# Attention and GEGLU backward, one decode step: weight rows put side by side in a partition, and what follows from it

## The chip, the cores and the metric

The kernel runs on one core of one Trainium2 chip. The time is the device time of one execution in microseconds (us), median of several executions. Engines as the profile names them: PE is the matrix engine (PEld its weight loads), DVE the vector engine, ACT the scalar engine, POOL the GpSimd engine, SP the engine that here only issues transfers. Transfers issued by SP show as queue q1, by ACT as q10, by POOL as q0.

## What is computed

The reference is one decode step of a block with attention and a GEGLU feed-forward side by side, and its gradients by the inputs and weights. The shapes: batch B = 4, D = 512, 32 query heads and 8 key/value heads of 128, a cache of 4096 positions of which the last W = 1024 are seen, F = 1792, all in bf16.

```python
xn = layernorm(x)                                  # x: [4, 1, 512]
q = (xn @ wq) as [4, 32, 1, 128]                   # wq: [512, 4096]
p = softmax(q @ k[:, :, -1024:].T * 128**-0.5)     # each kv head serves 4 query heads
o = p @ v[:, :, -1024:]
out = x + o @ wo + (gelu(xn @ w_gate) * (xn @ w_up)) @ w_down    # wo: [4096, 512]
# and, for grad_out dy: dx, dk_cache, dv_cache, dwq, dwo, dw_gate, dw_up, dw_down
```

The outputs are out (out_0), dx (out_1), dk and dv (out_2, out_3, both of the full cache's size, zero outside the window), dwq (out_4), dwo (out_5), dw_gate, dw_up, dw_down (out_6 to out_8). With do = dy @ wo.T by heads, dv comes from p and do, dp from do and v, dq from the scores' gradient and k, and dwo is the outer product of o and dy. 30.93 MB are read and 81.01 MB written, most of the latter the zeros of out_2 and out_3.

## The kernel before, in words

Weights and caches come into SBUF by SP (`load_w`, L228; `load_kv`, L235). The constants are made first: `xnT` and `dyT` (L204 to L210) hold the normalised x and dy with D on the partitions, in ND = 4 chunks of 128; chunk c holds the rows c*128 to c*128+127. `xnm` and `dym` (L213 to L218) hold xn and dy four times, each time with all but one row of each batch's 32-row group masked out; with them as an operand one matmul forms the outer product for one of the four heads of a group.

The feed-forward part runs first (L531 to L659): w_down transposed block by block for the gradient of the hidden layer, gate and up, the GELU's derivative, then w_gate and w_up transposed for dx. Outer products for the weight gradients are put as small pieces into a deque `bg`; `tick(n)` takes n pieces from it, and is called inside the loops, so that matmuls, evictions and stores of one part lie between those of the next. A piece is a matmul into a PSUM tile of pool `ps_w` (four slots, shared by nearly all tiles), an eviction by `evac` (L84), which picks ACT or DVE by a running account of costs, and after the last piece of a buffer a store issued by POOL.

Attention runs in NT = 4 stages t (L669 to L687), each with two kv heads, that is, HG = 8 query heads and CW = 1024 columns of w_q and rows of w_o. In a stage:

- `pre(t)` (L280) forms do and q for the stage. It transposes w_o in blocks (`woT_ps`, evicted by DVE as `woT`), multiplies them with `dyT` into `doq_ps` (L293), multiplies w_q with `xnT` into the other half of `doq_ps` (L298), spreads both (L305, L307) and transposes them back to rows (L313).
- `masks(t)` spreads these rows by batch on POOL.
- `scores(t, 0)` and `scores(t, 1)` (L327) transpose k and v blocks on PE (`T_ps`, evicted by DVE as `T_sb`) and form the scores and dp (`S_ps`, L341); `softmax`, `softmax_d` follow.
- `dvdk(t, k)` (L432) puts the pieces for dv and dk into `bg`.
- `odq(t, k)` (L408) forms o (k = 0) or dq (k = 1) in `od_ps`, evicts the rows (L421, L423), transposes them (L426) and copies the transposed (L428). For the next stage `pre(t + 1)` stands between `odq(t, 0)` and `odq(t, 1)`.
- `fin(t)` (L497) adds o @ w_o to the output's sum and dq @ w_q.T to that of dx, transposing w_q in blocks (L508).
- `load_next(t)` (L242) issues the loads of stage t + 2, whose w_o and w_q take the place of those that `fin(t)` has just read.
- `dw(t)` (L455) puts the pieces for dwo (`piece_o`) and dwq (`piece_q`) into `bg`.

The zeros of out_2 and out_3 are stored by ACT's queue from one zero tile, some at each of several places (`zeros`, L253).

The order on SP is the program's order; on the other engines a planner orders the instructions by priority and its own costs, and adds the waits. Two engines that use one PSUM tile are made to wait for each other.

How the rows of a weight lie on the partitions is set by the views of the loads, such as

```python
wo_v = A_wo.rearrange("(t h p) n -> t p h n", p=P, h=HG)         # L221
wq_v = A_wq.rearrange("(c p) (t j) -> t p c j", p=P, j=CW)       # L222
```

Partition p of w_o's tile holds the rows p, p + 128, ... p + 896 of the stage, eight runs of 1 KB; that of w_q four runs of 2 KB, that of w_gate and w_up four of 3.5 KB.

Of the kernel before, what the change touches and what calls it, by code (L numbers as in the profile page):

```python
# [14 lines left out]
P = 128  # L15
# [3 lines left out]
def kernel(  # L19
# [23 lines left out]

    nc = tc.nc
# [21 lines left out]
    assert Sq == 1 and Dh == P and D == 512 and F % P == 0 and RG == 32 and JQ * NQ == J and WQ == JQ * P  # L66
# [53 lines left out]
    nc.sync.dma_start(out=wg_sb[:], in_=B_w_gate.rearrange("(c p) f -> p c f", p=P))  # L120
    wu_sb = ffn_w.tile([P, ND, F], BF16, name="wu_sb")
    nc.sync.dma_start(out=wu_sb[:], in_=B_w_up.rearrange("(c p) f -> p c f", p=P))
# [83 lines left out]
    for src, dstT in ((dy_b, dyT), (xn_b, xnT)):  # L206
        tps = ps_x.tile([P, ND, P], BF16, name="tps", tag="x")
        for c in range(ND):
            nc.tensor.transpose(tps[:, c, :], src[:, c * P:(c + 1) * P], ident[:])
        nc.vector.tensor_copy(out=dstT[:], in_=tps[:].rearrange("p c (b r) -> p c b r", b=B)[:, :, :, 0])  # L210
# [3 lines left out]
    dym = const.tile([P, rep, D], BF16, name="dym")  # L214
# [6 lines left out]
    wo_v = A_wo.rearrange("(t h p) n -> t p h n", p=P, h=HG)  # L221
    wq_v = A_wq.rearrange("(c p) (t j) -> t p c j", p=P, j=CW)  # L222
# [57 lines left out]
    def pre(t):  # L280

        wo_sb, wq_sb = wo_t[t], wq_t[t]
        dq_ps = ps_x.tile([P, 2, HG, B], FP32, name="doq_ps", tag="x")
        for h2 in range(HG // 2):
# [6 lines left out]
            for i in range(2):  # L291
                for c in range(ND):
                    nc.tensor.matmul(dq_ps[:, 0, 2 * h2 + i, :], lhsT=woT[:, i, c, :], rhs=dyT[:, c, :],  # L293
                                     start=(c == 0), stop=(c == ND - 1))
            tick(2)
        for h in range(HG):
            for c in range(ND):
                nc.tensor.matmul(dq_ps[:, 1, h, :], lhsT=wq_sb[:, c, h * Dh:(h + 1) * Dh], rhs=xnT[:, c, :],  # L298
                                 start=(c == 0), stop=(c == ND - 1))
        T4 = []  # L300
        for k, (sc, zt, nm) in enumerate(((None, dom_all[t % 2], "do"), (scale, qm_all[t % 2], "qs"))):
            xT4 = attw.tile([P, NQ, B, HG], BF16, name=nm + "T4", tag=nm + "T4")
            src = dq_ps[:, k].rearrange("p h b -> p b h").unsqueeze(1).broadcast_to([P, NQ, B, HG])
# [104 lines left out]
    def odq(t, k):  # L408
# [10 lines left out]
        rows = attw.tile([P, GP, Dh], BF16, name="od_r", tag=f"od_r{k}")  # L419
        if k == 0:  # L420
            nc.vector.tensor_copy(out=rows[:], in_=od_ps[:, k])  # L421
        else:
            nc.scalar.activation(out=rows[:], in_=od_ps[:, k], func=ACT.Copy, scale=scale)  # L423
# [3 lines left out]
        rT = attw.tile([P, GP, rep, B], BF16, name="od_T", tag=f"od_T{k}")  # L427
        nc.vector.tensor_copy(out=rT[:],  # L428
                              in_=T_ps[:].rearrange("p g (b r) -> p g r b", b=B)[:, :, 0:rep, :])
        st[t][("o", "dq")[k]] = rows, rT  # L430
# [24 lines left out]
    def dw(t):  # L455

        o_r, dq_r = st[t]["o"][0], st[t]["dq"][0]

        def piece_o(g, i, held):
# [3 lines left out]
            nc.tensor.matmul(mps[:], lhsT=o_r[:, g, :], rhs=dym[:, i, :], start=True, stop=True)  # L463
            evac(held["osb"][:, i, :], mps[:], 512)
            if i == rep - 1:
                r0 = (t * HG + g * rep) * Dh
                store(nc.gpsimd, out=out_5[r0:r0 + rep * Dh, :].rearrange("(h p) n -> p h n", p=P),
                                    in_=held["osb"][:], kind="rest",
                          apart=["zeros", "rest"])

        def piece_q(c2, k, held):
# [5 lines left out]
            for i in range(2):  # L477
                nc.tensor.matmul(mps[:, i].rearrange("p g d -> p (g d)"),  # L478
                                 lhsT=xnm[:, i2 * 2 + i, c * P:(c + 1) * P],
                                 rhs=dq_r[:].rearrange("p g d -> p (g d)"), start=True, stop=True)  # L480
            evac(held["osb"][:, ci, :, i2 * 2:(i2 + 1) * 2, :], mps[:].rearrange("p i g d -> p g i d"), 512)
            if k == 3:
                store(nc.gpsimd, out=out_4[c2 * 2 * P:(c2 + 1) * 2 * P, t * CW:(t + 1) * CW].rearrange("(c p) j -> p c j", p=P),
# [13 lines left out]
    def fin(t):  # L497
# [3 lines left out]
        acc_sum(0, [(lambda c, h=h: wo_sb[:, h, c * P:(c + 1) * P], oT[:, h // rep, h % rep, :]) for h in range(HG)])  # L501
# [114 lines left out]
    def piece_g(s_r, og, c, i, held):  # L616
# [4 lines left out]
        nc.tensor.matmul(mps[:, 0:n, :].rearrange("p f d -> p (f d)"), lhsT=xnm[:, i, c * P:(c + 1) * P],  # L621
                         rhs=s_r[:, 0:n, :].rearrange("p f d -> p (f d)"), start=True, stop=True)
        evac(held["osb"][:, 0:n, i, :], mps[:, 0:n, :], n * P)
        if i == 3:
            store(nc.gpsimd, out=og[c * P:(c + 1) * P, :],
# [36 lines left out]
    with tc.tile_pool(name="stage", bufs=3, reuse_waits="tile") as stage, \  # L662
# [32 lines left out]
        for o in range(2):  # L695
# [3 lines left out]
            fin_ps.append(f_ps[:].rearrange("p c d -> p (c d)"))  # L699
        acc_o, acc_d = fin_ps  # L700
# [51 lines left out]
```

## Time and profile before

| | us |
|---|---|
| median of 3 runs (lowest, highest) | 290.51 (288.97, 291.4) |
| the profiled execution's own time | 289.23 |
| its span, first to last instruction | 287.5 |

| engine | busy us | share of the span |
|---|---|---|
| PE | 206.9 | 72% |
| PEld | 141.5 | 49% |
| DVE | 144.9 | 50% |
| ACT | 113.7 | 40% |
| POOL | 66.7 | 23% |

112.38 MB pass through the 16 DMA engines, 391 GB/s over the span; the mean granted clock of PE is 0.849 of full speed.

How to read the lines that follow: a group's line has line, engine, operation, output <- inputs, shape, count, then busy us and mean ns of one, then the idle time of the engine just before and what ended it. The chain that ended last is followed back from the end: each piece is what released the next. A window's line has the busy us and the number of instructions of each engine in that stretch, the granted PE clock, the share of the DMA engines and GB/s. A share slightly over 1 is counted where packets overlap.

### The profile page before, as it was taken

How to read it: one execution, taken by the hardware profiler on the slowest of the kernel's cores; microseconds unless marked ns; L12 is line 12 of the kernel's file. 1: busy time of each engine (PE TensorE's matmuls, PEld its weight loads, DVE VectorE, ACT ScalarE, POOL GpSimd, SP SyncE). 2: the span in 40 equal slices, each digit the busy share in tenths (PEclk: the TensorE clock that was granted, in tenths of full speed). 3: DMA queues.
4: the chain of work that ended last, by engine and by line, in shares of the span. 5: the costliest groups of instructions: out<-in, count | busy, mean ns of one | idle time of the engine just before them, and what ended most of it. 6: DMA issues, size and time to landing. Idle time of an engine off the chain costs nothing.

```text
span 287.5 us, 6821 instructions
## 1 busy us (share of the span) xinstructions
PE 206.9 (72%) x2956; PEld 141.5 (49%) x2956; DVE 144.9 (50%) x310; ACT 113.7 (40%) x217; POOL 66.7 (23%) x84
## 2 busy tenths in 40 slices
PE   1397994983977999545689996546998679597710
PEld 0386882652644765333357654323665355364310
DVE  5484572333564567312626674126476525537770
ACT  1201653443442467312424563134355444336610
POOL 7000130441303152311033323110252132112410
PEclk9996899597897899795958898959799969959975
DMA  5999999999999999999998999999999999999897
GB/s 138 381 389 376 385 399 421 413 403 429 423 426 427 413 372 401 435 415 427 416 419 330 327 363 429 426 427 411 415 413 380 395 390 412 406 415 360 337 393 295
DMA packets 30182, 112.38 MB, mean 391 GB/s; under 512 B 1537, under 2 KB 7689, under 8 KB 26057
## 3 DMA queue, kind: packets, MB, share of 16 engines
q10 hardware_dynamic: 4612, 50.46, 41.9%
q1 hardware_dynamic: 17732, 30.81, 29.4%
q0 software_dynamic: 7808, 30.67, 27.3%
q8 instruction: 23, 0.38, 0.5%
q14 instruction: 7, 0.05, 0.0%
HBM read 30.93 MB, written 81.01 MB: 389 GB/s over the span
## 4 chain that ended last, share of the span: by engine, by line
PE 47%; DMA 28%; DVE 14%; issue 4%; ACT 2%; POOL 1%; SPq 0%; DVEq 0%; ACTq 0%; POOLq 0%
DMA out_dram<-osb_o 14%; PE T_ps L336 9%; PE kv_ps L444 7%; DMA out_dram<-stg_dv 4%; DVE T_sb L94 4%; PE S_ps L341 4%; DMA wd_sb<-in_B_w_down_dram 4%; DMA out_dram<-osb_d 3%; PE od_ps L416 3%; PE woT_ps L288 3%; PE wqT_ps L508 3%; DMA out_dram<-osb_g 2%; PE acc_ps L181 2%; PE wgT_ps L648 2%; PE wdT_ps L536 2%
## 5 line engine op out<-in xcount | busy, mean ns | idle before, releaser
L94 DVE COPY T_sb<-T_ps 128x1024 bf16<-128x1024 bf16 x64 | 44.2, 691 | 34.2 <-PE T_ps L336 33.7
L92 ACT CAST stg_dv<-kv_ps 128x512 bf16<-128x512 f32 x52 | 28.8, 589 | 43.2 <-PE kv_ps L444 42.8
L92 ACT CAST stg_dk<-kv_ps 128x512 bf16<-128x512 f32 x46 | 25.0, 588 | 15.4 <-PE kv_ps L444 13.1
L336 PE MATMUL T_ps<-ident,vb 128*128 128x128 bf16 x256 | 26.1, 251 | 6.6 <-DVE osb_q L94 6.6
L336 PEld LDWEIGHTS <-vb 128*128 128x128 bf16 x256 | 20.0, 114 | 12.7 <-issue 8.9
L92 ACT CAST osb_q<-dwq_ps 128x512 bf16<-128x512 f32 x25 | 13.6, 589 | 30.4 <-DMA out_dram<-osb_o 20.1
L336 PE MATMUL T_ps<-ident,kb 128*128 128x128 bf16 x256 | 24.4, 228 | 0.5 <-ACT stg_dk L92 0.3
L336 PEld LDWEIGHTS <-kb 128*128 128x128 bf16 x256 | 18.1, 101 | 12.4 <-issue 5.0
L444 PE MATMUL kv_ps<-domr,P_q 128*128 128x512 bf16 x64 | 23.9, 435 | 0.0
L444 PE MATMUL kv_ps<-qmr,dS_q 128*128 128x512 bf16 x64 | 20.9, 410 | 1.5 <-ACT stg_dk L92 1.0
L92 ACT CAST osb_g<-dwg_ps 128x384 bf16<-128x384 f32 (+1 forms) x30 | 14.5, 534 | 17.6 <-PE dwg_ps L621 8.1
L94 DVE COPY woT<-woT_ps 128x1024 bf16<-128x1024 bf16 x16 | 11.1, 692 | 17.2 <-PE woT_ps L288 17.2
L478 PE MATMUL dwq_ps<-od_r,xnm 128*128 128x256 bf16 x64 | 12.5, 320 | 6.8 <-DVE osb_q L94 6.6
L352 POOL TENSOR_TENSOR dS_q<-dS_b,qmsk 128x1024 bf16<-128x1024 bf16 x4 | 7.5, 1884 | 34.3 <-DVE dS_b L405 34.3
L92 ACT CAST osb_o<-dwo_ps 128x512 bf16<-128x512 f32 x23 | 12.7, 588 | 7.0 <-PE dwo_ps L463 6.8
L341 PE MATMUL S_ps<-T_sb,dom 128*32 128x256 bf16 x128 | 10.5, 310 | 5.1 <-DVE T_sb L94 5.1
L98 POOL DMA_DIRECT2D out_dram<-osb_q x8 | 5.8, 731 | 34.6 <-ACT osb_q L92 34.6
L94 DVE COPY wqT<-wqT_ps 128x1024 bf16<-128x1024 bf16 x16 | 11.0, 687 | 5.5 <-PE wqT_ps L508 5.3
L508 PEld LDWEIGHTS <-wq_sb 128*128 128x128 bf16 x128 | 11.1, 120 | 5.3 <-issue 4.3
L94 DVE CAST osb_q<-dwq_ps 128x512 bf16<-128x512 f32 x7 | 4.7, 689 | 16.9 <-DMA out_dram<-osb_o 16.9
L98 POOL DMA_DIRECT2D out_dram<-stg_dv x8 | 6.2, 774 | 30.4 <-ACT stg_dv L92 30.4
L94 DVE CAST stg_dk<-kv_ps 128x512 bf16<-128x512 f32 x18 | 12.0, 685 | 2.4 <-PE kv_ps L444 1.2
(187 smaller groups left out, 381.1 us busy)
## 6 DMA issues: line engine op xcount, KB each, us to landing
out_dram<-ztile ACTq DMA_DIRECT2D x8, 3072.0 KB, 16.5
out_dram<-ztile ACTq DMA_DIRECT2D x16, 1536.0 KB, 15.3
kb<-in_A_k_cache_dram SPq DMA_DIRECT2D x8, 1024.0 KB, 17.1
vb<-in_A_v_cache_dram SPq DMA_DIRECT2D x8, 1024.0 KB, 49.5
out_dram<-stg_dv POOLq DMA_DIRECT2D x8, 1024.0 KB, 10.1
out_dram<-stg_dk POOLq DMA_DIRECT2D x8, 1024.0 KB, 8.4
wo_sb<-in_A_wo_dram SPq DMA_DIRECT2D x4, 1024.0 KB, 10.2
wq_sb<-in_A_wq_dram SPq DMA_DIRECT2D x4, 1024.0 KB, 14.2
```

Source lines behind the costliest of these rows:

```text
L92: last.append(nc.scalar.copy(out=out, in_=in_))
L94: return nc.vector.tensor_copy(out=out, in_=in_)
L98: d = eng.dma_start(out=out, in_=in_)
L181: nc.tensor.matmul(ps[:, c, :], lhsT=lf(c), rhs=rhs, start=(k == 0), stop=(k == len(terms) - 1))
L288: nc.tensor.transpose(wT_ps[:, i, c, :], wo_sb[:, 2 * h2 + i, c * P:(c + 1) * P], ident[:])
L336: nc.tensor.transpose(T_ps[:, j, :], blks[(t, g)][:, b, j, :], ident[:])
L341: nc.tensor.matmul(ps[q * RG:(q + 1) * RG, :], lhsT=lf[:, s * RG:(s + 1) * RG], rhs=T_sb[:, q * WQ:(q + 1) * WQ], start=(g == 0 and b == 0 ...
L352: nc.gpsimd.tensor_tensor(out=dst[:], in0=src[:].unsqueeze(1).broadcast_to([P, NQ, WQ]), in1=qmsk[:].unsqueeze(2).broadcast_to([P, NQ, WQ] ...
L416: nc.tensor.matmul(od_ps[b * RB:b * RB + rep, k, g, :], lhsT=pT[:, jj, c0:c0 + rep], rhs=blks[(t, g)][:, b, j, :], start=(j == 0), stop=(j ...
L444: nc.tensor.matmul(mps[:].rearrange("p b d -> p (b d)"), lhsT=src[:, q, jj * P:(jj + 1) * P], rhs=mr[:, g].rearrange("p b d -> p (b d)"), ...
L478: nc.tensor.matmul(mps[:, i].rearrange("p g d -> p (g d)"), lhsT=xnm[:, i2 * 2 + i, c * P:(c + 1) * P], rhs=dq_r[:].rearrange("p g d -> p ...
L508: nc.tensor.transpose(wT_ps[:, i, c, :], wq_sb[:, c, h * Dh:(h + 1) * Dh], ident[:])
```

## The change

The rows that one partition holds become neighbours in DRAM: row p*8 + k of a stage's w_o, and p*4 + c of w_gate, w_up and w_q, so that w_o has one run of 8 KB per partition, w_gate and w_up one of 14 KB; w_q keeps runs of 2 KB, as its columns are cut by stage. Every operand that meets such a weight follows: `xnT` is made from every fourth column, the outer products take every fourth column of `xnm`, the stores of out_4 to out_7 use the same order, and the final sum for dx is read in that order.

For w_o the rows of a block no longer belong to one head: block k holds the elements p*8 + k. So do is now formed as four rows, one per batch: `dyT` is the weight operand (4 columns) and `woT` streams, two blocks and 64 positions at a time, 128 columns. PE writes the results with a step of 8 words, so that the elements of a row lie in order. The rows are evicted (`do_row`, one half by ACT, one by DVE) and eight small transposes bring them back to head by head columns (`doT_ps`). q is formed as before, in a tile of its own (`dq_ps`). For dwo and the output, o is spread in `odq(t, 0)`: four masked copies of `od_ps`, by DVE and ACT in turn, into `X`, ordered by k, so that its columns fit block k; `oT` comes from eight matmuls with `qmsk`; `piece_o` multiplies a column block of `X` with `dy_b` itself, and `dym`, now needed by the feed-forward part alone, moves to that part's pool.

```diff
-    wg_sb: in_=B_w_gate.rearrange("(c p) f -> p c f", p=P)     # wu_sb alike
+    wg_sb: in_=B_w_gate.rearrange("(p c) f -> p c f", p=P)
-            nc.tensor.transpose(tps[:, c, :], src[:, c * P:(c + 1) * P], ident[:])
+            nc.tensor.transpose(tps[:, c, :], src[:, c:D:ND] if adj else src[:, c * P:(c + 1) * P], ident[:])
-    dym = const.tile([P, rep, D], BF16, name="dym")
+    dym = ffn.tile([P, rep, D], BF16, name="dym")
-    wo_v = A_wo.rearrange("(t h p) n -> t p h n", p=P, h=HG)
-    wq_v = A_wq.rearrange("(c p) (t j) -> t p c j", p=P, j=CW)
+    wo_v = A_wo.rearrange("(t p k) n -> t p k n", p=P, k=HG)
+    wq_v = A_wq.rearrange("(p c) (t j) -> t p c j", p=P, j=CW)
...
     def pre(t):
-        dq_ps = ps_x.tile([P, 2, HG, B], FP32, name="doq_ps", tag="x")
+        do_row = attw.tile([B, CW], BF16, name="do_row", tag="do_row", bufs=1)
+        do_ps = [pool.tile([B, P // 2, HG], FP32, name="do_ps", tag=tag) for pool, tag in ((ps_x, "x"), (ps_w, "w"))]
...
-            for i in range(2):
-                for c in range(ND):
-                    nc.tensor.matmul(dq_ps[:, 0, 2 * h2 + i, :], lhsT=woT[:, i, c, :], rhs=dyT[:, c, :],
+            for c in range(ND):
+                for u in range(2):
+                    nc.tensor.matmul(do_ps[u][:, :, 2 * h2:2 * h2 + 2].rearrange("b p k -> b k p"), lhsT=dyT[:, c, :],
+                                     rhs=woT[:, :, c, u * (P // 2):(u + 1) * (P // 2)],
                                      start=(c == 0), stop=(c == ND - 1))
             tick(2)
+        for u in range(2):
+            evac(do_row[:, u * (CW // 2):(u + 1) * (CW // 2)], do_ps[u][:].rearrange("b p k -> b (p k)"), 512,
+                 eng=("act", "dve")[u])
+        dq_ps = ps_w.tile([P, HG, B], FP32, name="dq_ps", tag="w")
...
+        doT_ps = ps_w.tile([P, HG, B], BF16, name="doT_ps", tag="w")
+        for h in range(HG):
+            nc.tensor.transpose(doT_ps[:, h, :], do_row[:, h * Dh:(h + 1) * Dh], ident[0:B, 0:B])
...
     def odq(t, k):
         if k == 0:
-            nc.vector.tensor_copy(out=rows[:], in_=od_ps[:, k])
+            X = attw.tile([P, HG, GP, rep, P // HG], BF16, name="o_x", tag="o_x", bufs=1)
+            for i in range(rep):
+                src = od_ps[:, 0].rearrange("p g (e k) -> p k g e", k=HG)
+                if i % 2:
+                    nc.scalar.activation(out=X[:, :, :, i, :], in_=src, func=ACT.Copy, scale=msk_i[:, i:i + 1])
+                else:
+                    nc.vector.tensor_scalar(out=X[:, :, :, i, :], in0=src, scalar1=msk_i[:, i:i + 1], scalar2=None,
+                                            op0=ALU.mult)
+            X = X[:].rearrange("p k g i e -> p k (g i e)")
+            oT_ps = ps_w.tile([P, HG, B], FP32, name="oT_ps", tag="w")
+            for h in range(HG):
+                nc.tensor.matmul(oT_ps[:, h, :], lhsT=X[:, h, :], rhs=qmsk[:], start=True, stop=True)
+            oT = attw.tile([P, HG, B], BF16, name="oT", tag="oT")
+            nc.vector.tensor_copy(out=oT[:], in_=oT_ps[:])
+            st[t]["o"] = X, oT
+            return
...
     def piece_o(g, i, held):
-            nc.tensor.matmul(mps[:], lhsT=o_r[:, g, :], rhs=dym[:, i, :], start=True, stop=True)
+            nc.tensor.matmul(mps[:], lhsT=X[:, g * rep + i, :], rhs=dy_b[:], start=True, stop=True)
...
-                r0 = (t * HG + g * rep) * Dh
-                store(nc.gpsimd, out=out_5[r0:r0 + rep * Dh, :].rearrange("(h p) n -> p h n", p=P),
+                store(nc.gpsimd, out=out_5[t * CW:(t + 1) * CW, :].rearrange("(p k) n -> p k n", k=HG)[
+                    :, g * rep:(g + 1) * rep, :], in_=held["osb"][:], kind="rest",
...
     def piece_q(c2, k, held):          # and piece_g
-                                 lhsT=xnm[:, i2 * 2 + i, c * P:(c + 1) * P],
+                                 lhsT=xnm[:, i2 * 2 + i, c:D:ND],
...
-        acc_sum(0, [(lambda c, h=h: wo_sb[:, h, c * P:(c + 1) * P], oT[:, h // rep, h % rep, :]) for h in range(HG)])
+        acc_sum(0, [(lambda c, h=h: wo_sb[:, h, c * P:(c + 1) * P], oT[:, h, :]) for h in range(HG)])
...
-        acc_o, acc_d = fin_ps
+        acc_o, acc_d = fin_ps[0].rearrange("p c d -> p (c d)"), fin_ps[1].rearrange("p c d -> p d c")
```

## The prediction

> **What bounds the kernel now.** I read the page's slices first, then the DMA queues, then the chain that ended last, then windows of 5 us around the places where the transfers thin out, then the order of instructions there.
>
> The slices and the queues, from the page (the first line is the busy share of the DMA engines in tenths, the last three the queues: packets, MB, share of 16 engines):
>
> ```profile
> DMA  5999999999999999999998999999999999999897
> q10 hardware_dynamic: 4612, 50.46, 41.9%
> q1 hardware_dynamic: 17732, 30.81, 29.4%
> q0 software_dynamic: 7808, 30.67, 27.3%
> ```
>
> The DMA engines are full in nearly every slice. The three queues add up to 98.6% of 287.5 us, so the end is close to the DMA work plus the time in which the engines had nothing. The loads (q1) have by far the most packets for their bytes. The trace's packet records say what size costs what: on q1, 6024 packets of 1 KB at a mean of 50.7 ns (median 46), 10240 of 2 KB at 87.4 (84), 1024 of 3.5 KB at 145.8; on q0, 6592 of 4 KB at 168.4 and 512 of 7 KB at 273.4; on q10, 4096 of 12 KB at 467.6. From the same records the time without work, as a mean over 16 engines, is 3.7 us at the start, 1.3 us at the very end, and only 3.6 us between: 0.06 at 100 to 110 us, 1.5 at 150 to 170, 0.7 at 215 to 225, 1.3 at 260 to 275.
>
> The chain that ended last, in order of time (start, us, what), shows that compute is not simply hidden:
>
> ```profile
> 40.30 8.98 DMA out_dram<-osb_d
> ...
> 113.48 17.92 DMA out_dram<-osb_o
> 131.53 0.70 DVE osb_q L94
> ...
> 170.73 19.11 DMA out_dram<-osb_o
> 189.96 0.70 DVE osb_q L94
> ...
> 252.06 12.71 DMA out_dram<-stg_dv
> ```
>
> After each load of the next weights comes a stretch set by DMA (a store must land before its buffer is used again), and from 131.5 to 170.7 and from 190.0 to 252.1 a stretch of PE, DVE and ACT work. The windows of the second hand-over (us, busy time and count of PE, PEld, DVE, ACT, POOL, then clock, DMA share, GB/s):
>
> ```profile
> 145.00:150.00 5.00, 5.00 (x91) 3.33 (x84) 0.84 (x2) 1.36 (x3) 1.43 (x2) 0.53 1.04 436
> 150.00:155.00 5.00, 4.40 (x97) 3.23 (x96) 3.00 (x6) 2.83 (x6) 0.59 (x1) 1.00 0.89 353
> 155.00:160.00 5.00, 5.00 (x58) 3.66 (x55) 3.42 (x10) 2.51 (x5) 3.74 (x3) 0.66 0.91 280
> ```
>
> Here pre(2), odq(1, 1) and fin(1) run. PE is busy 14.4 of 15 us, partly at a clock of 0.53 and 0.66, and DMA falls to 0.89 and 280 GB/s: by the packet records the zeros in q10 end at about 151 us, and the next loads wait for fin. So **each hand-over is set by PE**, and what comes after it by DMA. Both count.
>
> **What the change takes away: packets.** w_o falls from 4096 packets of 1 KB to 512 of 8 KB, if a partition's contiguous run becomes one packet as the 12 KB rows of q10 are. 4096 x 50.7 ns / 16 is 13.0 us. An 8 KB packet lies between the rows of 7 KB (273) and 12 KB (468), in proportion 312 ns: 512 x 312 / 16 = 10.0 us. Saved 3.0 us, 0.75 for each of the four loads. w_gate and w_up fall from 1024 packets of 3.5 KB (9.3 us) to 256 of 14 KB, at 468 x 14/12 = 546 ns 8.7 us: 0.6 saved. Lower end: the medians of 1 and 2 KB (46, 84) leave 8 ns for a packet beside its bytes, and 4352 packets x 8 / 16 is 2.2 us. So **2.2 to 3.6 us of DMA work**. w_q still has 2 KB runs and w_down and out_8 are as before: nothing. The stores of out_5 leave as 4 KB packets already, now one run each: between nothing and 1024 x 8.4 ns / 16 = 0.5 us saved (168.4 against the median of 160); I take nothing.
>
> Not all of it reaches the end. Half (w_gate, w_up, w_o of stages 0 and 1: 2.1 us) falls before about 55 us, where the feed-forward part keeps PE the bound until 39.4; only the stretch of 8.98 us gets shorter, I take 0.7. The w_o of stages 2 and 3 come right after the first two hand-overs, in DMA's stretches: 0.75 each, whole. **-2.2 us.**
>
> **What it adds, stage by stage.** The rows (timeline: start, us; then groups: busy, mean ns, idle before; then a wait: us, times, longest):
>
> ```profile
> 145.27 1.03 PE L288 MATMUL woT_ps<-ident,wo_sb 128*128 128x128 bf16 x8
> 152.36 0.35 PE L293 MATMUL doq_ps<-dyT,woT 128*128 128x4 bf16 x8
> ```
>
> ```profile
> L421 DVE CAST od_r<-od_ps 128x256 bf16<-128x256 f32 x4 | 1.7, 422 | 3.6 <-PE od_ps L416 3.6
> L423 ACT ACTIVATE od_r<-od_ps 128x256 bf16<-128x256 f32 x4 | 1.6, 388 | 4.3 <-PE od_ps L416 4.3
> ```
>
> ```profile
> ACT qsT L307 <- DVE doT L305: 3.8, 3, 1.4
> ```
>
> (a) do as rows. 32 matmuls per stage stay 32, but stream 128 columns instead of 4. Eight of the old take 0.35 to 0.40 us. Eight that stream 128 columns take 0.55 to 0.61 in the transposes at full clock and 1.03 at the clock of 0.53. I take 0.58: 4 x (0.58 - 0.36) = **+0.9 us**; the other end is 4 x (1.03 - 0.36) = 2.7. Their results go into PSUM with a step of 8 words. No PE instruction of this trace writes PSUM with a step. Nearest rows: DVE's reads of doq_ps with a step of 4 words (L305, 128 elements, 292 ns) cost what 256 packed bf16 elements cost (L94 PT, 292 ns), so a step shows no price there; from above, a matmul of 512 columns (two kv_ps in 0.60) bounds a step that costs four times: 32 x (0.30 - 0.07) = 7.4 us a stage; a step may also cost less than nothing only if fewer columns counted, which the unchanged count of 128 excludes. I take none, by L305.
>
> [...]
>
> (b) The way back. Two evictions of 4 x 512 (0.59 on ACT, 0.69 on DVE by the forms of L92 and L94) lie beside the 32 matmuls of L298 (0.80 to 0.94 us), so they cost nothing; if ACT or DVE has an eviction in front, 0.6 shows. Eight small transposes at 44 ns (the rate of L293): +0.35. ACT's wait of 3.8 us for DVE's read of the same tile goes, since dq_ps and doT_ps are now two tiles; late next is the do arm, so nothing is gained. Taken **+0.35**, ends 0 and 1.
>
> (c) do_ps holds one of the four ps_w slots through pre, and dq_ps and doT_ps one each at its end. Behind a PE that waits for a slot stand all its transposes. Ends 0 and 1.2 us (four times half an eviction of 0.69); PE already had 96% work there, so I take **+0.15**.
>
> (d) o spread by head: four reads of od_ps (DVE 422, ACT 388 ns, by turns) instead of one. The wait of L307 shows that ACT does not read a tile that DVE is reading, so they come one after another: 1.6 us instead of 0.4, and DVE stands in its queue for 0.8 us more, with T_sb evictions behind it, on which PE's next scores wait. Half of it is covered by T_sb already delivered: **+0.4**, ends 0 and 1.5. The 8 matmuls of oT (0.35) replace two transposes (0.27) and a copy of the same size.
>
> (e) Weights read with a step of 8 bytes (xnm for out_4, out_6, out_7; xn_b): no row shows stepped weights; bounds 0 and a doubled load, 96 x 0.11 = 10 us of PEld over the kernel, beside matmuls of 320 ns and more: taken as nothing. The final reads of f_ps in another order (0.55 to 0.75 us each) end at 280, five us before the last store: nothing. One buffer for X: written at 136 for stage 1, last read at 116 for stage 0: nothing. dym moved: its last reader is the same dwd_ps matmul for which the loads of stage 1 already wait: nothing.
>
> Sum: per hand-over 0.9 + 0.35 + 0.15 + 0.4 = 1.8, times three 5.4; the first pre lies half beside the 8.98 us wait, +0.3; the last o, +0.1. **+5.8 - 2.2 = +3.6 us.** The profiled execution took 289.23 us (span 287.5 and 1.7 around it), 1.3 below the median of 290.51; on the median's base 290.5 + 3.6 = **294.1 us**.
>
> **The rivals.**
> 1. The stepped PSUM writes are slow: half a 512-column matmul instead of 0.07, +0.08 x 32 = 2.6 us on each of three hand-overs, 7.7 in all on top: 301.8. For it: nothing but the absence of a row. Against: the read rows.
> 2. The other side: everything added lies beside DMA, and the packets decide. For it: DMA full in 37 of 40 slices, 98.6% booked. It decides from the point where a hand-over's delay is below what still stands in the queues; the 0.06 us of idle at 100 to 110 says that this is nearly so there. Price: -2.2 to -3.6, middle -2.9: 287.6, and down to 286.9.
> 3. Half and half: the hand-overs lose 2 to 3 us and the packets give 2.2 to 3.6 back: 290.5.
> 4. The long runs are cut into 4 KB packets again, so that little is saved: 1024 x 168.4 / 16 = 10.8 against 13.0 still saves 2.2. This lies inside the ranges above.
>
> **How the numbers follow.** Forecast 0.38 (0.30 of it above 1%), rival 1 0.17, rival 2 0.22 (0.17 of it below -1%), rival 3 with 4 in it 0.23 (0.18 within 1%, 0.03 above, 0.02 below). Slower by over 1%: 0.50; within 1%: 0.31; faster: 0.19. One per cent, 2.9 us, is also about what this kernel's runs (288.97 to 291.4) can tell from no change. The range runs from rival 2's 286.9 to just short of rival 1's 301.8: 286.9 to 300.5. Likeliest case by itself: 291.5 to 297.
>
> **What would show it.** q1 should have about 13400 packets instead of 17732 and a share about 1% lower; w_o should land in about 9.5 us instead of 10.2. Windows at the hand-overs should show PE at 5.0 of 5 for longer, and DMA's idle time there grown by 1 to 2 us each; the do matmuls, eight in 0.55 to 0.65 at full clock. Eight in over 0.9 at full clock is rival 1. DMA at 1.0 through the hand-overs and an end 3 us earlier is rival 2. What would make me wrong beyond these: another order of PE's instructions, since the planner places the new ones by its own costs.

## The result and the profile after

The changed kernel takes **307.23 us** (median of 4 runs, 305.01 to 309.61) against 289.92 for the kernel before on the same chip: ratio **1.0567**, 95% interval 1.045 to 1.0684, some 16 us slower. The ratios, here and below, leave out executions that ran in a slower state, so they can differ a little from the quotient of the medians. The forecast was 294.1 with a range of 286.9 to 300.5. The direction held, the size didn't.

The page of the changed kernel, the lines that answer to those shown of before (DMA slices, then the three queues: packets, MB, share of 16 engines):

```profile
DMA  5999999999999979999986799999982998999895
q10 hardware_dynamic: 4612, 50.46, 39.6%
q1 hardware_dynamic: 13380, 30.81, 28.0%
q0 software_dynamic: 7808, 30.67, 25.5%
```

The packets fell as worked out (q1 has 13380), but the shares now add up to 93.1% instead of 98.6%, and the slices have holes where there were hardly any. They lie at 106 to 114, 152 to 175 and 220 to 235 us, at the three hand-overs. By the packet records of loads and stores, the 16 engines were busy for 277.6 us (before 277.4), and idle up to the last packet for 23.0 (before 8.5). So nearly the whole loss is **idle time of the DMA engines**: 2.5 us from 100 to 115 (at the same hand-over before 0.06), 6.2 from 155 to 175 (1.5), 6.8 from 220 to 235 (0.7). The last packet ends at 300.6 instead of 285.9.

The windows of the second hand-over (PE, PEld, DVE, ACT, POOL, clock, DMA share, GB/s):

```profile
150.00:155.00 5.00, 4.88 (x73) 3.67 (x72) 1.20 (x2) 1.55 (x4) 0.15 (x1) 0.64 1.00 414
155.00:160.00 5.00, 4.30 (x37) 2.76 (x37) 2.26 (x4) 2.07 (x5) 0.00 (x0) 1.00 0.63 250
160.00:165.00 5.00, 5.00 (x96) 4.04 (x96) 2.48 (x8) 1.77 (x5) 1.53 (x2) 0.89 0.59 207
165.00:170.00 5.00, 4.83 (x58) 3.54 (x56) 3.27 (x5) 2.94 (x6) 2.96 (x2) 0.77 0.66 220
```

PE is busy 19 of 20 us, while DMA stands at about 0.6 in the last three windows: by the packet records the zeros in q10 end at about 154 us, and the next loads wait for `fin`. The same stretch in the order of PE's instructions, at the first hand-over; first the kernel before (timeline: start, us, instruction):

```profile
92.31 0.61 PE L288 MATMUL woT_ps<-ident,wo_sb 128*128 128x128 bf16 x8
93.70 0.35 PE L293 MATMUL doq_ps<-dyT,woT 128*128 128x4 bf16 x8 [0.35 <-DVE woT L94]
93.92 0.61 PE L288 MATMUL woT_ps<-ident,wo_sb 128*128 128x128 bf16 x8
...
94.79 0.56 PE L288 MATMUL woT_ps<-ident,wo_sb 128*128 128x128 bf16 x7
95.31 0.35 PE L293 MATMUL doq_ps<-dyT,woT 128*128 128x4 bf16 x8
```

then the changed one:

```profile
89.45 1.87 PE L297 MATMUL do_ps<-woT,dyT 128*4 128x128 bf16 x8 [0.27 <-DVE woT L96]
92.07 0.67 PE L292 MATMUL woT_ps<-ident,wo_sb 128*128 128x128 bf16 x8
93.54 1.04 PE L297 MATMUL do_ps<-woT,dyT 128*4 128x128 bf16 x8
94.50 0.62 PE L292 MATMUL woT_ps<-ident,wo_sb 128*128 128x128 bf16 x8
95.91 1.03 PE L297 MATMUL do_ps<-woT,dyT 128*4 128x128 bf16 x8
...
100.28 0.35 PE L311 MATMUL doT_ps<-ident,do_row 4*128 4x4 bf16 x8
```

Eight do matmuls take 1.03 us at full clock and 1.87 at half; 0.58 was forecast, and "over 0.9 at full clock" was the mark of rival 1. A second thing shows: before, a block pair comes every 1.6 us, and at the first two hand-overs the last pair's transposes (94.79) start ahead of the do matmuls of the pair before (95.31); now no pair's transposes do, and one comes every 2.37 us. From the first transpose of w_o to the first q matmul, stages 1 to 3, `pre` takes 11.1, 12.0 and 11.9 us (before 8.2, 8.5 and 8.2). Up to the end of the last transpose of w_q in `fin`, behind which the next load of w_q stands, it is 18.7, 19.4 and 19.4 us (before 14.5, 15.1 and 13.5). The three differences add up to 14.4 us, of the 16.1 by which the profiled executions differ.

### The profile page after: what moved, and what is told of

The parts are those of the page before. It is cut to its first block, busy times and chain, and to the rows that moved or that the text cites. A ratio compares the mean times of both kernels' runs of the same rounds, so it can differ in the third digit from the quotient of the medians.

```text
span 303.6 us, 6950 instructions
## 1 busy us (share of the span) xinstructions
PE 225.6 (74%) x3012; PEld 156.3 (52%) x3012; DVE 150.5 (50%) x318; ACT 119.2 (39%) x229; POOL 65.4 (22%) x84
## 3 DMA queue, kind: packets, MB, share of 16 engines
q1 hardware_dynamic: 13380, 30.81, 28.0%
## 4 chain that ended last, share of the span: by engine, by line
PE 52%; DMA 25%; DVE 12%; issue 3%; ACT 3%; POOL 1%; SPq 0%; DVEq 0%; ACTq 0%; POOLq 0%
PE T_ps L348 10%; PE kv_ps L471 8%; DMA out_dram<-osb_o 8%; PE do_ps L297 5%; DMA out_dram<-stg_dv 4%; PE S_ps L353 4%; DMA wo_sb<-in_A_wo_dram 4%; DMA wd_sb<-in_B_w_down_dram 3%; DMA out_dram<-ztile 3%; DVE T_sb L96 3%; PE wqT_ps L534 3%; PE wgT_ps L674 3%; DMA out_dram<-osb_g 2%; PE acc_ps L183 2%; PE od_ps L428 2%
## 5 line engine op out<-in xcount | busy, mean ns | idle before, releaser
L348 PE MATMUL T_ps<-ident,vb 128*128 128x128 bf16 x256 | 27.7, 260 | 14.5 <-DVE osb_q L96 7.7
L348 PEld LDWEIGHTS <-vb 128*128 128x128 bf16 x256 | 21.4, 118 | 21.8 <-issue 18.5
L94 ACT CAST osb_q<-dwq_ps 128x512 bf16<-128x512 f32 x25 | 13.5, 590 | 32.7 <-DMA out_dram<-osb_o 12.9
L471 PE MATMUL kv_ps<-domr,P_q 128*128 128x512 bf16 x64 | 24.7, 453 | 0.1
L348 PE MATMUL T_ps<-ident,kb 128*128 128x128 bf16 x256 | 23.0, 220 | 0.3 <-ACT osb_g L94 0.2
L96 DVE COPY woT<-woT_ps 128x1024 bf16<-128x1024 bf16 x16 | 11.1, 692 | 24.4 <-PE woT_ps L292 24.4
L471 PE MATMUL kv_ps<-qmr,dS_q 128*128 128x512 bf16 x64 | 21.9, 426 | 1.5 <-ACT stg_dk L94 1.1
L297 PE MATMUL do_ps<-woT,dyT 128*4 128x128 bf16 x128 | 19.0, 342 | 3.3 <-DVE woT L96 3.2
L94 ACT CAST osb_g<-dwg_ps 128x512 bf16<-128x512 f32 (+1 forms) x30 | 14.5, 537 | 17.5 <-PE dwg_ps L647 6.8
L348 PEld LDWEIGHTS <-kb 128*128 128x128 bf16 x256 | 17.0, 98 | 8.3 <-issue 0.6
L297 PEld LDWEIGHTS <-dyT 128*4 128x4 bf16 x128 | 14.8, 128 | 7.2 <-issue 6.8
L534 PE MATMUL wqT_ps<-ident,wq_sb 128*128 128x128 bf16 x128 | 13.5, 265 | 0.0
## 6 DMA issues: line engine op xcount, KB each, us to landing
out_dram<-ztile ACTq DMA_DIRECT2D x16, 1536.0 KB, 15.1
```

The source lines that it names most:

```text
L94: last.append(nc.scalar.copy(out=out, in_=in_))
L96: return nc.vector.tensor_copy(out=out, in_=in_)
L297: nc.tensor.matmul(do_ps[u][:, :, 2 * h2:2 * h2 + 2].rearrange("b p k -> b k p"), lhsT=dyT[:, c, :], rhs=woT[:, :, c, u * (P // 2):(u + 1) ...
L348: nc.tensor.transpose(T_ps[:, j, :], blks[(t, g)][:, b, j, :], ident[:])
L471: nc.tensor.matmul(mps[:].rearrange("p b d -> p (b d)"), lhsT=src[:, q, jj * P:(jj + 1) * P], rhs=mr[:, g].rearrange("p b d -> p (b d)"), ...
L534: nc.tensor.transpose(wT_ps[:, i, c, :], wq_sb[:, c, h * Dh:(h + 1) * Dh], ident[:])
```

## The experiments

Each ratio is to the kernel before, run on the same chip in turns, with its 95% interval. A point is 0.01 of the ratio, about 2.9 us; the difference of two rows of the table is uncertain by some 0.5 to 1.6 points.

| kernel | ratio | interval |
|---|---|---|
| changed | 1.0567 | 1.045 to 1.0684 |
| e1: changed, PSUM written packed | 1.0155 | 1.0062 to 1.0247 |
| e4: changed, second half of do in another bank | 1.0357 | 1.0254 to 1.046 |
| e14: e1 and e4 together | 1.0103 | 1.0031 to 1.0174 |
| e14p: e14, w_o in 1 KB packets | 1.0102 | 1.0046 to 1.0158 |
| e15: changed, w_o in 1 KB packets | 1.0494 | 1.0413 to 1.0576 |
| e6: changed, written in pairs of words | 1.0563 | 1.0528 to 1.0599 |
| e2: before, new order of gate, up, q | 1.0001 | 0.9961 to 1.0041 |
| e8: e2 and new order of w_o, no new work | 1.0147 | 1.009 to 1.0204 |
| e9: e8, w_o in 1 KB packets | 1.0072 | 1.0026 to 1.0118 |
| e10: e8, out_5 stored in the old order | 1.0134 | 1.0081 to 1.0186 |
| e3: before, o spread alone | 1.0017 | 0.9987 to 1.0048 |
| e5: before, do as packed rows, o spread | 1.0061 | 1.0015 to 1.0106 |
| e12: e5, second half of do in another bank | 1.0016 | 0.9981 to 1.005 |
| e16: e2 and e12, that is, all but w_o's order | 0.996 | 0.9927 to 0.9993 |

### The PSUM writes

**e1**, the step moved from PE's write to the read of the eviction; the order of the instructions is the same on every engine.

```diff
-        do_ps = [pool.tile([B, P // 2, HG], FP32, ...
+        do_ps = [pool.tile([B, HG, P // 2], FP32, ...
-    nc.tensor.matmul(do_ps[u][:, :, 2 * h2:2 * h2 + 2].rearrange("b p k -> b k p"), ...
+    nc.tensor.matmul(do_ps[u][:, 2 * h2:2 * h2 + 2, :], ...
-    evac(do_row[...], do_ps[u][:].rearrange("b p k -> b (p k)"), 512, ...
+    evac(do_row[...].rearrange("b (p k) -> b p k", k=HG), do_ps[u][:].rearrange("b k p -> b p k"), 512, ...
```

> The changed kernel, but PE writes do packed (64 results side by side) and the eviction into do_row does the interleaving by reading PSUM with a step; every engine issues the same instructions in the same order. Theory S (the stepped PSUM write is the main cost): eight do matmuls fall from 1.03 us to 0.55 to 0.65 at full clock, 0.4 us for each of 4 pairs of blocks, more where the clock is halved; the stretch from the first w_o transpose to the first q matmul falls from 11.1 to 12.0 us by 1.6 to 2.5, and the time from 307 by three to four times that, to 298 to 302. Theory O (the row form and the order that the planner finds for it cost, the step hardly): the matmuls get shorter but PE then waits for woT, and the time stays above 304. Evictions: 0.57 and 0.68 us as before if a stepped read costs nothing, above 1 us if it does.

Measured: 297.14 us, ratio 1.0155. The groups of the do matmuls by form, changed and then packed (busy us, mean ns of one, idle before):

```profile
L297 PE MATMUL do_ps<-woT,dyT 128*4 128x128 bf16 x128 | 19.0, 342 | 3.3 <-DVE woT L96 3.2
```

```profile
L297 PE MATMUL do_ps<-woT,dyT 128*4 128x128 bf16 x128 | 11.3, 240 | 3.2 <-DVE woT L96 2.9
```

From one start to the next, a matmul of 128 columns takes 55 ns packed and 109 stepped at full clock, 107 and 213 at half: the step halves the rate, at either clock. The evictions that now read with the step cost what they did (0.58 us on ACT, 0.68 on DVE, with and without it). So the write is the cause and not the interleaving as such: 4.1 points, about 12 us by the ratios, 10.4 between the two profiled executions. The time lies just below the 298 to 302 of theory S.

That is more than the matmuls themselves. In a stage three groups at full clock and one at half cost 3 x (1.03 - 0.61) + (1.87 - 1.01) = 2.1 us, 6.4 for the three hand-overs. Most of the rest is seen after `pre`, in the transposes of w_q for which the next load waits (timeline of PE in `fin`, second hand-over); changed:

```profile
163.96 1.06 PE L471 MATMUL kv_ps<-qmr,dS_q 128*128 128x512 bf16 x2
164.81 1.06 PE L534 MATMUL wqT_ps<-ident,wq_sb 128*128 128x128 bf16 x8
```

with packed writes:

```profile
158.99 0.59 PE L472 MATMUL kv_ps<-qmr,dS_q 128*128 128x512 bf16 x2
159.42 0.61 PE L535 MATMUL wqT_ps<-ident,wq_sb 128*128 128x128 bf16 x8
```

and in the kernel before:

```profile
157.05 1.06 PE L444 MATMUL kv_ps<-qmr,dS_q 128*128 128x512 bf16 x2
157.90 1.06 PE L508 MATMUL wqT_ps<-ident,wq_sb 128*128 128x128 bf16 x8
```

From the first to the last transpose of w_q it takes 4.9, 5.0 and 5.0 us at the three hand-overs of the changed kernel and 3.5, 3.6 and 3.6 with packed writes. Each of the longer stretches (4.9 us and more) has 3.4 us at a granted clock of 0.5, the shorter ones have none. **That is 4.2 us in instructions that the edit doesn't touch**; with the 6.4 of the matmuls it is about what the profiled executions differ by. But the kernel before, with its shorter `pre`, has this stretch at half clock as well, at two of the three hand-overs (5.1, 5.0 and 3.6 us). So against the kernel before the changed one loses by it at the third hand-over alone, 1.4 us, and the packed kernel gains at the first two. The length of `pre` doesn't decide it: 8.2 and 8.5 us before with half clock behind them, 9.4 to 10.2 with packed writes without. What sets the clock there no run shows, nor whether it follows from the write or only happens to fall so. The 4.1 points hold both.

**e6**, the same PSUM words, but the columns streamed position by position, so that two neighbouring words are written before each step.

```diff
-    nc.tensor.matmul(do_ps[u][:, :, 2 * h2:2 * h2 + 2].rearrange("b p k -> b k p"), lhsT=dyT[:, c, :],
-                     rhs=woT[:, :, c, u * (P // 2):(u + 1) * (P // 2)],
+    nc.tensor.matmul(do_ps[u][:, :, 2 * h2:2 * h2 + 2], lhsT=dyT[:, c, :],
+                     rhs=woT[:, :, c, u * (P // 2):(u + 1) * (P // 2)].rearrange("p k q -> p q k"),
```

> The changed kernel with one edit: the do matmuls stream their 128 columns position by position, the two blocks of a position side by side, instead of one block after the other. The same 128 values go to the same PSUM words with the same count of instructions; only now two neighbouring words (8 bytes) are written one after the other before each step of 8 words, where the changed kernel steps by 8 words after every word. The orders of the other engines stay as they are. Theory A (the single word per step is what costs): eight matmuls fall from 1.03 to about 0.61 us, as packed, and the time to that of the packed write, ratio to the kernel before 1.016, 294 to 298 us. Theory B (every step costs its share, so half as many steps cost half): eight take about 0.82 us and the ratio is 1.03 to 1.04. Theory C (any write that is not one run costs the same, or the moving operand, now read with jumps of 1 KB, costs as much): eight stay at 1.03 us or more, ratio 1.05 to 1.06. [...]

Measured: 306.07 us, ratio 1.0563, in the range of theory C, of which the second half (the moving operand) fits better than the first. The last two groups of one `pre` (timeline):

```profile
99.04 1.15 PE L297 MATMUL do_ps<-woT,dyT 128*4 128x128 bf16 x8
101.52 1.15 PE L297 MATMUL do_ps<-woT,dyT 128*4 128x128 bf16 x8
```

All sixteen groups take 1.14 to 1.15, 123 ns from start to start, whether the granted clock is 1.00 or, as at 212.6 us, 0.50. At half clock that is far less than the 213 ns of single words, so two words in a run were cheaper to write there than two apart. At full clock 123 is more than the 109 of single words. What holds 123 ns at either clock no run shows: it doesn't follow PE's clock, and the jumps of 1 KB in the moving operand, the only other thing in the edit, weren't timed alone. The step moved from the write to the moving operand was no gain (ratio 1.0563, changed 1.0567).

### The slot

**e4**, the second half of do in a bank that is free at that time, so that it holds none of the four ps_w slots.

```diff
-   ... for pool, tag in ((ps_x, "x"), (ps_w, "w"))]
+   ... for pool, tag in ((ps_x, "x"), (ps_a, "S"))]
```

> The changed kernel, but the second half of do_ps takes the bank of the score sums, which is free at that time, so that ps_w keeps its four slots through pre. Theory C (the slot held through pre makes PE wait): the stretch from the first w_o transpose to the first q matmul falls by 1 us or more in each stage and the time to 301 to 304. Theory S: nothing changes in the do matmuls, 0 to 1 us a stage: 304 to 308.

Measured: 301.94 us, ratio 1.0357, with eight stepped matmuls still at 1.03. Some of the next pair's transposes stand ahead of the last one's do matmuls again, at each of the three hand-overs. So the slot costs 2.1 points of the changed kernel, by the order in which PE's work can be placed.

**e14**, both edits.

> The changed kernel with both edits at once: do written packed into PSUM (the step moved to the eviction's read), and the second half of do in another bank than the four ps_w slots. The step alone was worth 4.1 points of the ratio, the slot alone 2.1. If they are separate causes that add up, the ratio is 1.0567 x (1.0155/1.0567) x (1.0357/1.0567) = 0.995, 289 to 291 us, and the cores' queues lose nothing at the hand-overs. If both only mend the same wait (PE behind a slot while the matmuls are slow), the second edit brings nothing once the first is made: ratio 1.01 to 1.02, 294 to 297 us. In between, 1.00 to 1.01, some of the waits are shared; the loop over the four block pairs of w_o then shows 8.5 to 9 us (11.1 to 12.0 changed, 8.2 to 8.5 before).

Measured: 294.14 us, ratio 1.0103, in the range in which both mend the same wait. Beside packed writes the slot is worth 0.5 points instead of 2.1, which the intervals don't tell from nothing. `pre` does get shorter (7.0, 8.5 and 8.6 us, with the slot held 9.4, 9.7 and 10.2), but at the first two hand-overs what stands behind it gets longer by as much: up to the last transpose of w_q it is 15.7, 15.6 and 14.4 us against 15.5, 15.7 and 16.2. One point over the kernel before is left.

### The parts that I had booked at little or nothing

**e3**, in the kernel before, o spread as in the change's `odq(t, 0)` (the same four masked copies, but heads in the old order), `oT` by eight matmuls, `piece_o` with `dy_b`.

```diff
-            nc.vector.tensor_copy(out=rows[:], in_=od_ps[:, k])
+            for i in range(rep):          # DVE and ACT in turn
+                nc.vector.tensor_scalar(out=X[:, :, i, :], in0=od_ps[:, 0], scalar1=msk_i[:, i:i + 1], ...
-            nc.tensor.matmul(mps[:], lhsT=o_r[:, g, :], rhs=dym[:, i, :], start=True, stop=True)
+            nc.tensor.matmul(mps[:], lhsT=X[:, g * rep + i, :], rhs=dy_b[:], start=True, stop=True)
```

> The kernel before with the spread of o alone: four masked copies of od_ps by DVE and ACT in turn, oT from eight matmuls with qmsk, dwo from X and dy_b, dym in the feed-forward part's pool; rows of the weights and do as before. My step (d) says +0.4 us per hand-over, +1.3 in all: ratio 1.003 to 1.006. If it is hidden: 0.998 to 1.002. With the rows of do packed it was 1.006 in the old layout, so above 1.006 it would be the whole of that, and the rows of do would cost nothing.

Measured: 290.31 us, ratio 1.0017, as if hidden; at most 1.4 us.

**e5**, e3 and do as rows, written packed, head by head:

```diff
-    nc.tensor.matmul(dq_ps[:, 0, 2 * h2 + i, :], lhsT=woT[:, i, c, :], rhs=dyT[:, c, :], ...
+    nc.tensor.matmul(do_ps[h // 4][:, h % 4, :], lhsT=dyT[:, c, :], rhs=woT[:, i, c, :], ...      # h = 2 * h2 + i
```

> All of the change but the row order: loads, stores and outer products as before, do formed as rows by 128-column matmuls written packed and transposed back, o spread by head into masked copies for dwo. Theory S: without the step the row form costs 0.2 us a pair of blocks and 0.4 a stage for the way back, the spread 0.4: 3 to 5 us over before, ratio 1.010 to 1.018, since no packets are saved. Theory O: the row form costs as much here as in the changed kernel, ratio above 1.035.

Measured: 293.82 us, ratio 1.0061, below both theories: without the step the row form costs less than I had worked out. **e12** is e5 with e4's edit of the bank:

> The rows of do and the spread of o in the old layout (1.0061 by itself), with the second half of do in another bank than the four ps_w slots. My step (c) says 0.15 us per hand-over, so no change that can be seen: 1.004 to 1.008. If the slot is what the row form costs: 0.998 to 1.002, as the spread alone (1.0017).

Measured: 291.5 us, ratio 1.0016. The rows of do, their way back and the spread together cost nothing that can be measured (at most half a point), so long as the write is packed and the slots are left alone. The 0.45 points between e5 and e12 by themselves are within their intervals.

### The row order and the packets

**e2**, in the kernel before the new order of w_gate, w_up and w_q, with all that follows (`xnT`, `xnm[:, i, c:D:ND]`, stores, final sum).

```diff
-    wg_sb: in_=B_w_gate.rearrange("(c p) f -> p c f", p=P)     # wu_sb, wq_v alike
+    wg_sb: in_=B_w_gate.rearrange("(p c) f -> p c f", p=P)
```

> The kernel before, with w_gate, w_up and w_q in the new row order (weights of the outer products read with a step of four, stores of dwq, dw_gate and dw_up and the final sum in that order), w_o and all that hangs on it as before; every engine keeps its order. My theory: 768 packets fewer, 0.6 us of DMA work at most, stepped weights free: 289 to 290.5, ratio 0.995 to 1.003. Rival: the stepped weights of dwq, dw_gate and dw_up or the scattered stores cost: their weight loads would take 0.2 us instead of 0.11 and the ratio would be above 1.01, up to a third of the 17 us.

Measured: 290.62 us, ratio 1.0001. The weight loads with a step of 8 bytes take 113 to 120 ns (medians) instead of 98, beside matmuls of 270 and more: hidden.

**e8**, e2 with w_o loaded in 8 KB runs and out_5 stored in the new order; the engines' instructions and their order are those of e2. What follows from the new order for do and o is left out, so what is computed from w_o belongs to other rows; the work is the same in count and shape.

```diff
-    wo_v = A_wo.rearrange("(t h p) n -> t p h n", p=P, h=HG)
+    wo_v = A_wo.rearrange("(t p k) n -> t p k n", p=P, k=HG)
-                store(nc.gpsimd, out=out_5[r0:r0 + rep * Dh, :].rearrange("(h p) n -> p h n", p=P), ...
+                store(nc.gpsimd, out=out_5[t * CW:(t + 1) * CW, :].rearrange("(p k) n -> p k n", k=HG)[:, g * rep:(g + 1) * rep, :], ...
```

> The kernel before with all the loads and stores of the change (w_o in one 8 KB run per partition, w_gate and w_up in one of 14 KB, the stores of out_4 to out_7 in the new row order, xnT and xnm by every fourth column) and none of the new work on do and o. So the meaning of w_o's blocks isn't followed: what is computed from w_o and for out_5 belongs to permuted rows; the work is the same in count and shape. My step on the packets says -2.2 us (1.5 to 3.6 between): ratio 0.988 to 0.995, 287 to 289 us. The rival says that the DMA work hardly falls, as the packet records of the changed kernel show (the 2 KB packets dearer, 91 ns instead of 87), or that other work hides it: ratio 0.997 to 1.003, 290 to 292 us.

Measured: 294.39 us, ratio 1.0147: neither theory. Fewer packets made it **slower**, with no new work at all. The chain that ended last (start, us, what), e2 first:

```profile
42.55 9.86 DMA out_dram<-osb_d
...
113.57 17.89 DMA out_dram<-osb_o
```

then e8:

```profile
40.72 13.09 DMA out_dram<-osb_d
...
115.01 19.59 DMA out_dram<-osb_o
```

The two stores that PE waits for take 3.2 and 1.7 us longer, and land 1.4 and 3.1 us later, while w_o lands earlier (8.0 us after its issue instead of 10.3). From 36 to 61 us the DMA engines are full in both, with a share of 1.00 to 1.05 in every window, so what the loads get sooner the stores would get later; that is my reading of it. SP's timeline fits (start, us in issue); e2:

```profile
42.75 12.86 SPq L238 DMA_DIRECT2D kb<-in_A_k_cache_dram  x1
```

and e8:

```profile
40.86 1.00 SPq L238 DMA_DIRECT2D kb<-in_A_k_cache_dram  x1
```

In e2, where w_o goes in 1024 packets, the load of the next k block stands 12.9 us in issue; in e8, where it goes in 128, it passes in 1.0 us, and 1 MB more of loads is in the queue beside the store. By the packet records the DMA work itself fell, the busy time of the engines from 278.1 to 276.7 us; their idle time rose from 7.5 to 11.4, for the most part at the first two hand-overs.

**e9**, e8 with w_o in 1 KB packets, by rows of 528 elements in the tile.

```diff
-        wo_t[t] = pool.tile([P, HG, D], BF16, name="wo_sb", tag="wo")
-        nc.sync.dma_start(out=wo_t[t][:], in_=wo_v[t])
+        wo_t[t] = pool.tile([P, HG, D + 16], BF16, name="wo_sb", tag="wo")
+        nc.sync.dma_start(out=wo_t[t][:, :, 0:D], in_=wo_v[t])
```

> The layouts alone again (the work from w_o still belongs to permuted rows), with one edit: the tile of w_o has rows of 528 instead of 512 elements in SBUF, so that the 8 KB run of a partition can't move as one piece and goes as eight packets of 1 KB as in the kernel before. Row order in DRAM, the stores of out_5 and the order of every engine's instructions are those of the layouts alone (1.0147). Theory P (the large packets of w_o do the harm: the loads take a larger share of the DMA engines, and the stores that PE waits for land later): ratio back at 0.997 to 1.003, w_o lands in about 10.3 us again instead of 8.0, q1 16964 packets. Theory S (the stores of out_5 in their new order, or the new row order itself, do the harm): the ratio stays at 1.010 to 1.018.

Measured: ratio 1.0072, between the theories, its interval overlapping that of e8. The store of osb_d is back at 9.50 us in the chain. It doesn't go by the packet size alone, though: with 8 KB packets it takes 11.52 us in e10 and 9.14 in e14. And w_o, in 1 KB packets again, doesn't land as late as before (page, KB each and median us to landing; e2, then e9):

```profile
wo_sb<-in_A_wo_dram SPq DMA_DIRECT2D x4, 1024.0 KB, 10.3
```

```profile
wo_sb<-in_A_wo_dram SPq DMA_DIRECT2D x4, 1024.0 KB, 8.7
```

Whether it is the place of the rows that makes it land sooner isn't shown: in e5, with the rows and packets of the kernel before, it is 8.6 us, in e1, with 8 KB packets, 9.5. The landing of w_o depends on more than its packets.

**e10**, e8 with the stores of out_5 as before.

> The layouts alone again (the work from w_o still belongs to permuted rows), with the stores of out_5 in the order of the kernel before (four rows 128 apart per partition) and w_o loaded in 8 KB runs. Theory P (the large packets of w_o do the harm): ratio 1.010 to 1.018, as for all the layouts together (1.0147). Theory S (the new order of out_5's stores does it): 0.997 to 1.003.

Measured: 294.22 us, ratio 1.0134, by theory P. The stores' order isn't it.

**e14p** is e14 with e9's edit of the tile, **e15** the changed kernel with the same edit.

> The changed kernel with packed PSUM writes and the second half of do in another bank (1.0103 by itself), and w_o in 1 KB packets by the wider tile rows. Theory P and separate causes: the 1.5 points of the large packets go as well, 1.0103 - 0.0147 = 0.996, 287.5 to 290.5 us. If what is left at 1.0103 is the row form itself (0.6 points in the old layout): 1.004 to 1.008, 291 to 292.5 us. If the packets do no harm in this kernel: 1.010, 293 us.

> The changed kernel with one edit: the tile of w_o has rows of 528 elements in SBUF, so w_o goes in 1 KB packets as before the change; the order of the instructions is the same. My step on the packets would make it slower than the changed kernel (1.0567): 0.75 us for each load that counts, ratio 1.061 to 1.065. If the large packets harm as in the layouts alone (1.0147 against 1.0072): 1.042 to 1.050. If neither, because PE at the hand-overs sets the time: 1.053 to 1.060.

Measured: 293.56 us, ratio 1.0102, and 306.28 us, ratio 1.0494. With 8 KB packets they were 1.0103 and 1.0567. So the large packets bring no gain in either; whether they harm the changed kernel the intervals don't tell.

**e16**, all of the change except w_o's row order: e2 and e12 together.

> All of the change except the row order of w_o: w_gate, w_up and w_q in the new order, do as rows packed head by head (first half of the heads done after two of four block pairs), o spread, second half of do in another bank. Its parts alone: layouts of gate, up and q 1.0001, rows and spread with the other bank 1.0016. If what was left at 1.010 belongs to w_o's row order: 1.000 to 1.004, 289.5 to 291.5 us. If it comes from the new rows together with the new order of the other weights: 1.008 to 1.012, 292.5 to 293.5 us.

Measured: 289.82 us, ratio 0.996 (0.9927 to 0.9993), the only one below the kernel before, by about 1 us, and lower than forecast. Its DMA slices have no holes (page):

```profile
DMA  4999999999999999999999999999999999999897
```

What was left at 1.010 is w_o's row order and what hangs on it: 1.4 points from e16 to e14, and 1.5 from e2 to e8, where besides the row order only out_5's stores differ, which e10 clears. The step from e16 to e14 holds more: both halves of do become complete only with the last block, do and o are read from PSUM with a step, and PE's order is another.

## Why the prediction was wrong, step by step

From the changed kernel to the one before there is a way over the runs: packed writes 4.1 points, the slot 0.5, w_o's row order 1.4, and the rest of the change -0.4; in all 5.67. The parts are uncertain by 0.3 to 1.5 points each, and go by the order in which the edits were made: the slot alone was worth 2.1.

- **The bound: right.** "Each hand-over is set by PE, and what comes after it by DMA." The loss is DMA idle time at the three hand-overs, behind a busy PE. Forecast was 1 to 2 us of it each; it is 2.4, 4.7 and 6.1 more than before.
- **Step (a) is the one that failed: "a step shows no price there ... I take none, by L305".** The row was a read of PSUM by DVE; the operation was a write by PE. Reads with a step cost nothing here (e1's evictions, 0.58 and 0.68 us as in the changed kernel), PE's writes with a step ran at half rate: 109 ns against 55. The row that the range rested on told nothing of the thing in question: the step was taken as free by my estimate, and measured at 2.1 us a stage. Rival 1, with 2.6 per hand-over, came nearest to what happened; it had 0.17, and the range stopped just short of it.
- **The clock behind `pre` wasn't in any step.** I counted durations of instructions at the clock that they had, and the clock moved: the transposes of w_q in `fin` ran at half clock at two hand-overs before, at all three after, and at none with packed writes, 1.4 us each time. Why is open.
- **The -2.2 us of packets: wrong in sign.** The arithmetic of the records held for single sizes (8 KB: 339 ns, forecast 312; 14 KB: 543, forecast 546), but the 2 KB packets of q1 took 91 instead of 87 ns, and the busy time of the engines stayed at 277 to 278 us. Where the engines' work is the same (e2 and e8) it did fall, by 1.4 us, and the kernel still took 1.5 points longer, in idle time. w_o landed sooner (6.8 us, forecast 9.5). Counted as a gain, its new order was a loss. With rival 1's 301.8, taking back the 2.2 and adding some 4 us for w_o's order comes to 308, measured 307.2; but this sum is made afterwards and leaves out the slot, so its closeness is in part luck.
- **Step (c), the slot: under-sized.** 0.15 us was taken, 1.2 was the upper end; 2.1 points are 6 us, 2 per hand-over, beside stepped writes, and 0.5 points are 1.4 us, 0.5 per hand-over, beside packed ones, no more than the intervals. "Another order of PE's instructions" was named as what would make me wrong, but not priced: the slot kept the next transposes from going ahead.
- **Steps (b), (d) and (e): right, or a little high.** The eight small transposes take 0.35; the spread, taken as 1.3 us in all, 0.5 and at most 1.4 (1.0017); stepped weights and the final reads nothing (1.0001).
- **Rivals 2 and 3** rested on the packets' gain and fall with it (of the 40 slices that rival 2 cites, 36 are full, not 37); **rival 4** is out: the 8 KB and 14 KB runs went as single packets.

**What stays open.** Why w_o's row order costs 1.4 points: that its load takes more of the DMA engines while PE waits for a store is what the chains of e2 and e8 suggest, but in e14, which pays the 1.4 points too, the store of osb_d takes hardly longer than before (9.14 us, before 8.98), and small packets bring back only half in one kernel (e9) and none in another (e14p). Open is also what sets PE's clock behind `pre`. Whether another place for that load would turn its earlier landing into a gain wasn't tried.

## What to carry to other kernels

Let PE write PSUM in one run and put the step into the eviction's read: here that took the do matmuls from 109 to 55 ns and left the evictions at 0.58 and 0.68 us. A row that prices an access on one engine, or a read, says nothing of a write by another engine (a read of 292 ns by DVE priced PE's write at nothing, and that took 109 ns instead of 55): without a row of the same kind, the upper end is a case to be priced, not to be waved off. Where DMA is full and stores are waited for, a load that lands sooner need not be a gain: here fewer packets and a w_o that landed in 8.0 us instead of 10.3 came with a ratio of 1.0147. Before a difference between two kernels is put down to an edit, look for the same stretch in the kernel that it all began with: the half clock in `fin` was there already.

## What the runs showed that I hadn't expected

- The do matmuls that wrote single words of PSUM 32 bytes apart ran at half rate at full and at half clock (109 and 213 ns for 128 columns, packed 55 and 107); with two words in a run but a moving operand that jumps by 1 KB they took 123 ns at both.
- Stepped reads of PSUM by ACT and DVE took what packed ones did (0.58 and 0.68 us for 4 x 512 in both e1 and the changed kernel).
- The same transposes of w_q in `fin` fell into 3.4 us of half clock at two, three or none of the hand-overs of three kernels, at 1.4 us each; what decides it isn't known.
- 4352 packets fewer left the busy time of the DMA engines as it was (277.4 and 277.6 us).
